# Half of the q transposes of an attention and MLP kernel as copies between partition halves

## The chip, the core and the metric

The kernel runs on one core of one Trainium2 chip. The metric is the device time of one execution in microseconds. A core has a matrix engine (TensorE, PE in the profile; its weight loads are PEld), a vector engine (VectorE, DVE), a scalar engine (ScalarE, ACT), GpSimd (POOL), and SyncE (SP), whose queue here only issues DMAs. POOL issues the loads from memory. Each engine works through its own instructions in their order; semaphores make one engine wait for another, or for a DMA. On chip, data lie in SBUF with 128 partitions, and TensorE writes to PSUM banks.

## The reference

Eight batches of 12 heads, 448 positions, head size 64; then an MLP on all 8 x 448 = 3584 rows:

```python
scores = scale * np.matmul(q, k.transpose(0, 1, 3, 2))     # scale = 1/sqrt(64)
attn = np.maximum(scores, 0.0) ** 2 / S                    # S = 448, no softmax
attn_out = np.matmul(attn, v)                              # (8, 12, 448, 64)
x = attn_out.transpose(0, 2, 1, 3).reshape(B * S, H * D)   # (3584, 768)
h = x @ w_in                                               # w_in (768, 2048)
g = 0.5 * h * (1.0 + erf(h * inv_sqrt2))
out = g @ w_out                                            # w_out (2048, 768)
```

All inputs and the output are fp32. The kernel computes with bf16 inputs of the matmuls.

## The kernel before

**Attention.** A batch is split into 3 head groups of 4 heads. For each group there are 7 QK steps of four quarter-array matmuls (64x64 tiles, 448 columns, into `ps`, L748). Each step's result is evicted with relu and the scale, by ScalarE (L760) or VectorE (L762), and squared on VectorE (L769) into `a_sq`. When the 7 steps of a group are there, 28 matmuls (AV, into `pav`, L809) multiply by v, and the result is cast into `xT`. Then come the MLP's matmuls: `psh` (L861), `pb` (L1005) and `pso` (L1178), with their sums on VectorE (`osb`, `part`, `s_sb`) and gelu on ScalarE. While attention of batches 2 to 7 runs, MLP pieces of earlier batches fill TensorE between its steps.

**How q and k come.** POOL loads k, q and v of a batch with a cast to bf16 into `nk`, `nq` and `v_sb`. From batch 2 on, one pair of buffers `nq` and `nk` serves all batches, so the loads of the next batch may start only when the present batch has been transposed out of them. v has three buffers. QK needs q and k with the head's 64 entries on the partitions. For batches 0 and 1 TensorE transposes them. For batches 2 to 7, SP issues DMA transposes (`add_T_dma`, the DMA at L660): from 128 columns of `nq` or `nk` to the 128 partitions of `qT` or `kT`, which have two buffers each; a batch's transposes wait for the QK of two batches before (`old_T`).

`qT` is a row of slots of 112 columns. A DMA transpose turns 128 columns, that is two blocks of 64, into one slot: one block on partitions 0 to 63, the next on 64 to 127. QK needs every block on both halves, since its quarter-array tiles read the lower or the upper half. So `nq` is transposed twice, from two starting points 64 columns apart: the even transposes fill the slots 1, 3, 5, ..., the odd ones the slots 0, 2, 4, .... With both, the upper half has block s in slot s, and the lower half block s - 1. Per batch there are 9 DMA transposes on SP, in the order kT, even, odd for each of the three groups. An odd one covers 8 or 9 slots and reaches into the next group, so it also waits for that group's q load (`beyond`).

**Gates.** POOL's loads of the next batch overwrite what the transposes read. POOL waits for them with a small copy from the transposed tile (`gate`, 128x16): `add_gate` for q of a group (L701), `add_kgate` for kT (L716), `add_vgate` for the last batch's v (L709). In each batch POOL has, in order: gate of group 0, kT gate of group 2, the v load of the batch after next, gate of group 2, and then the six loads of k and q. `war` gives these loads the transposes as predecessors.

**Order.** All instructions are recorded first as operations with the engines that may run them and estimated costs (`sch.add`). `ORDER` (L83 to 163) is a list of words, an engine's letter and an operation's number, which fixes for all operations on which engine and in which order they stand. It was made from a planner's costs; when the kernel is built it is only replayed. Stores of the output (L1139) stand in SP's queue between the transposes, each as two DMAs.

Of the kernel before, what the change touches and what calls it, by code (L numbers as in the profile page):

```python
# [92 lines left out]
P219 D220 A244 A258 A178 D200 P267 D191 P259 P210 G148 A179 S229 P204 D197 A184 G150 A268 P186  # L93
A260 D182 D187 P263 D215 A211 D188 P261 G151 A205 P207 A264 P216 S230 G153 D206 D185 D224 A262
A217 P192 A208 G154 D193 D194 D209 D212 P247 D221 A248 P255 P143 D218 A256 P201 P225 A144 A226
G237 D202 D203 P265 D227 D380 S231 D386 S232 P245 S233 A266 P362 A246 P372 A363 P370 A373 A371
D390 D388 P356 P366 A357 P368 A367 P376 D389 A369 A377 P358 P364 D383 D381 A359 A365 P360 P350
A361 P354 A351 P288 P282 D387 D384 A355 A289 P294 P378 A295 P374 P276 S234 A379 G240 D283 D284
D382 G149 P279 A375 P291 D280 D385 S235 P348 P352 P285 A292 A277 A349 D296 D290 D286 D287 A353
P306 P303 S236 P392 P300 D393 A304 P342 P394 D395 P396 P398 D391 A307 D281 A343 P312 P315 G152  # L100
A397 A301 A313 G155 G242 D278 D293 D316 G269 P297 G270 D399 G271 G272 P327 P400 D298 P402 D314
D302 D427 P324 A299 A328 S408 P309 D401 D403 P336 P404 A325 S409 A310 A337 P431 D305 D317 D326
G273 P318 A432 P339 P333 P435 D428 A334 G274 S410 D405 D311 P433 S411 S406 A340 P447 D319 A448
D344 D308 P462 D320 P321 G417 D434 P330 D429 P437 A322 A436 D329 D430 D335 A331 D341 P439 A323
S412 D338 D332 S413 P459 A463 P453 P345 A454 D460 D438 D440 S414 S415 P474 P465 D475 D455 G420
P441 P443 D442 A346 A466 P486 D444 A347 D467 G275 S416 P450 D451 A487 P456 D452 P531 G423 A532
D570 P547 A548 P549 P545 A550 D457 D571 S407 A546 P498 D464 P489 P504 D449 P529 D461 P523 A499
A490 P477 G418 D458 P480 D505 D478 A530 G419 P468 S551 G421 S552 A481 P471 A524 D476 D482 D469
D472 P483 D572 D473 P527 A484 D488 P537 A528 P533 D506 P510 G422 D485 A470 A538 D491 A534 P507
P501 S553 D500 A511 G424 P539 A502 A508 G425 S554 S445 P519 P625 G560 A626 P513 D479 A520 P492  # L110
P495 D514 D512 S555 P616 S556 S557 A540 D493 D515 P525 D496 A617 A494 G563 P535 P619 S558 D509
A526 D627 G426 S559 P613 A536 D614 G566 P610 P543 A544 D615 P541 D503 P521 D497 D573 G561 P640
A620 A611 P646 A641 D647 P516 D517 P634 A522 A542 D642 S446 P628 P574 A635 D629 P576 G562 P670
D612 S714 D621 D630 A518 S715 G564 P622 D618 G565 A575 P664 A623 A671 P578 D577 P580 P661 P637
A665 D624 D581 A638 P631 P649 D662 P676 A579 S716 D639 P582 P584 A632 D633 P652 A677 D583 A650
P667 D636 A653 D585 D651 S717 D648 A668 D654 P643 A644 G567 P586 S718 S588 D590 P594 P779 D645
D587 P673 P655 A780 G568 D592 D591 A595 P658 A674 P596 P782 D666 A659 S589 S719 D597 P773 A783
P598 A774 P600 D656 S720 P815 D663 P785 D675 A599 D657 P776 D669 D672 A786 G723 A777 A816 D601
G726 D660 D775 P602 D678 P604 P809 D735 D593 P791 S721 D603 D605 P679 A810 P806 P606 S722 D781
A680 S608 D778 P692 D607 D681 D792 A807 G569 A693 P706 P788 D787 P797 P824 A707 P686 A687 P704  # L120
D789 D790 G729 P702 D784 G724 P830 A798 S877 D793 A825 D817 P812 P794 G725 D831 A705 P803 A813
A795 D804 P836 D805 S878 S609 A703 G727 G728 A837 P708 A796 S879 D814 S880 P712 P833 D808 P839
D811 D733 P800 A709 P682 D801 A713 D802 D826 D799 A834 S881 A683 P700 G730 G731 D840 P696 A701
P688 S882 P925 P934 A935 P818 A689 D926 A697 P922 D832 P821 A819 P694 D734 D736 D923 D841 A820
G886 A695 A822 P710 S883 A711 D823 P827 P940 D828 G889 P931 D835 D829 P698 S884 A941 A699 D838
P690 A932 P684 D927 P919 G732 A691 P928 A685 D920 P842 D924 D936 A929 S885 P916 A843 A917 P949
P737 G892 G887 P739 D930 A950 P955 G888 D921 D844 S988 P943 S989 D933 G890 G891 A738 A956 D740
D918 D944 P964 P741 P743 A742 P745 D744 A965 D942 D746 P747 P749 P952 D753 D951 P946 S990 D748
D953 P937 D750 A947 G893 D954 P982 P958 D754 P757 A758 P759 P761 D957 S751 S991 D938 A959 A983
P997 A939 D960 P973 A998 D755 P979 G894 D760 D948 S992 P763 A762 A974 P765 D966 D764 D999 P767  # L130
P967 S752 S993 G1441 G895 D756 D766 D945 P976 A980 S994 A977 D975 D968 P961 P1015 A1016 P1027 D768
D896 D1028 P769 D770 P871 D962 S995 P855 D898 D981 D978 A872 A963 P970 D971 A856 D1017 P1036 D984
P1000 P865 A1001 P849 A866 A1037 P857 P1006 D972 P1024 D1002 A850 D969 P985 A1025 P1009 D1007 A858
P1012 D1077 P875 P869 A876 P861 A1013 S996 D897 A870 D986 A862 P873 D899 A874 A987 D1038 D1010
P847 S771 P1057 A848 P1030 P1003 D1008 D1011 A1031 P853 D1069 D1058 A1004 P863 D1014 P1063 D1029
D1005 A864 P1018 P1021 A854 D1064 P1045 P859 A1022 A1019 D1032 D1073 A860 D1074 P845 P867 P1039
D1070 A1046 A846 A1020 D1023 D1078 A868 P1051 P1033 P851 A1034 D1035 A852 A1040 P902 D1026 D1047
P900 A1052 D1065 P1048 A901 D1041 D1053 D1059 P1060 A1061 D903 P1042 P1054 A1043 A1049 D1079 D1080
P904 A905 D1044 D1071 P906 D1062 A1055 P908 P1081 D1151 D907 S772 D909 D1056 P1083 P1098 A1099
P1100 D1076 P912 P910 D1149 D1150 A1082 D1050 P1066 D913 D911 S914 D1084 S915 P1085 D1072 D1101  # L140
P1153 A1067 A1068 P1102 A1154 D1075 P1087 D1152 P1104 A1086 D1189 P1089 A1103 D1190 P1106 D1088
P1155 D1105 D1090 P1092 D1107 A1091 D1191 P1109 A1108 D1156 P1095 P1112 D1093 P1115 D1110 A1094
P1132 D1096 A1111 P1117 D1113 A1097 P1134 D1192 A1116 A1133 P1157 A1114 D1118 P1119 D1135 P1136
A1158 P1121 P1138 A1120 P1123 A1137 P1140 D1122 P1159 D1139 D1124 P1126 D1141 A1125 P1143 A1142
D1160 P1129 P1146 D1127 P1161 D1144 A1128 D1130 A1145 P1163 D1147 A1131 D1301 A1148 D1162 D1302
P1165 D1169 D1164 S1167 P1173 D1170 D1166 S1168 P1175 D1171 D1174 P1177 D1172 D1176 D1303 P1179
D1304 A1178 P1181 D1180 P1183 D1263 D1182 P1185 D1261 D1184 S1187 P1193 D1262 P1210 D1186 S1188
P1195 D1264 P1212 A1194 A1211 P1265 D1196 P1197 D1213 P1214 A1266 P1199 P1216 A1198 P1201 A1215
P1218 D1200 P1267 D1217 D1202 P1204 D1219 A1203 P1221 A1220 D1268 P1207 P1224 D1205 P1227 D1222
A1206 P1244 D1208 A1223 P1229 D1225 A1209 P1246 A1228 A1245 P1269 A1226 D1230 P1231 D1247 P1248  # L150
A1270 P1233 P1250 A1232 P1235 A1249 P1252 D1234 P1271 D1251 D1236 P1238 D1253 A1237 P1255 A1254
D1272 P1241 P1258 D1239 P1273 D1256 A1240 D1242 A1257 P1275 D1259 A1243 A1260 D1274 P1277 D1281
D1276 S1279 P1285 D1282 D1278 S1280 P1287 D1283 D1286 P1289 D1284 D1288 P1291 D1290 P1293 D1292
P1295 D1375 D1294 P1297 D1373 D1296 S1299 P1305 D1374 P1322 D1298 S1300 P1307 D1376 P1324 A1306
A1323 P1377 D1308 P1309 D1325 P1326 A1378 P1311 P1328 A1310 P1313 A1327 P1330 D1312 P1379 D1329
D1314 P1316 D1331 A1315 P1333 A1332 D1380 P1319 P1336 D1317 P1339 D1334 A1318 P1356 D1320 A1335
P1341 D1337 A1321 P1358 A1340 A1357 P1381 A1338 D1342 P1343 D1359 P1360 A1382 P1345 P1362 A1344
P1347 A1361 P1364 D1346 P1383 D1363 D1348 P1350 D1365 A1349 P1367 A1366 D1384 P1353 P1370 D1351
P1385 D1368 A1352 D1354 A1369 P1387 D1371 A1355 A1372 D1386 P1389 D1393 D1388 S1391 P1397 D1394
D1390 S1392 P1399 D1395 D1398 P1401 D1396 D1400 P1403 D1402 P1405 D1404 P1407 D1415 D1406 P1409  # L160
D1413 D1408 S1411 P1417 D1414 D1410 S1412 P1419 D1416 D1418 P1421 D1420 P1423 D1422 S1433 P1425
D1424 P1427 D1426 S1434 P1429 D1428 S1435 P1430 D1431 S1436 D1432 S1437
"""


class Op:

# [227 lines left out]
def kernel(  # L395
# [317 lines left out]
    def add_kgate(b, g):  # L713

        def fn(e):
            nc.gpsimd.tensor_copy(gate, get_T(b)[1][:, g, :: NK * 8])  # L716
# [803 lines left out]
```

## Time and profile before

| | us |
|---|---|
| median of 3 runs | 367.81 (367.30 to 368.25) |
| the profiled execution's own time | 369.13 |
| its span, first to last instruction | 367.3 |
| TensorE busy | 356.4 |
| VectorE busy | 286.5 |
| ScalarE busy | 201.6 |
| POOL busy | 65.1 |
| DMA transposes: qT 36, kT 18, median to landing | 4.0 |

Times in the profile are counted from the span's start. The share of busy time is an average over stages: up to some 57 us attention of batches 0 and 1 and the weights, from 57 to about 250 us attention of batches 2 to 7 between MLP pieces, and then the MLP alone. Matmuls overlap, so a busy TensorE is not always at its peak. In a chain or a list of waits, "DMA qT<-nq" is the landing of a transpose. An instruction's duration on VectorE and ScalarE overlaps a little with the next one's.

### The profile page before, as it was taken

The numbers are of one execution on the slowest core, as the hardware profiler recorded it, in microseconds if no ns is written. First come the engines' busy times: TensorE is split into PE (matmuls) and PEld (weight loads), VectorE is DVE, ScalarE is ACT, GpSimd is POOL, SyncE is SP. The second block draws the span as 40 slices with busy tenths as digits, with TensorE's granted clock in tenths as the row PEclk, the third lists the DMA queues.
The fourth block names the chain that finished last, engine by engine and source line by source line (L and its number), as shares of the span: only waits on it lengthen the run. The fifth ranks groups of instructions, "written<-read, shape, count | busy, mean of one in ns | idle before, by whom it ended". The sixth has DMA issues, their size and how long they took to land.

```text
span 367.3 us, 8386 instructions
## 1 busy us (share of the span) xinstructions
PE 356.4 (97%) x3517; PEld 218.4 (59%) x3517; DVE 286.5 (78%) x480; ACT 201.6 (55%) x319; POOL 65.1 (18%) x104
## 2 busy tenths in 40 slices
PE   7899999999999999899999999999999999999995
PEld 3566565455544454454455545467885897688663
DVE  3998887389899888688997898799778558755863
ACT  4997754676757676658672656763540353045200
POOL 8655700070150150060150100000000000000000
PEclk9999999999999999999999999999999999999999
DMA  9999999899999999999999970002002301310222
GB/s 169 200 202 204 202 204 187 172 161 188 177 175 188 188 181 148 230 168 214 179 159 193 186 169 2 0 2 73 15 2 87 87 2 34 95 46 0 87 86 86
DMA packets 89700, 47.25 MB, mean 129 GB/s; under 512 B 55360, under 2 KB 86336, under 8 KB 89664
## 3 DMA queue, kind: packets, MB, share of 16 engines
q0 software_dynamic: 32912, 22.47, 42.2%
q1 hardware_dynamic: 56112, 23.76, 33.8%
q8 instruction: 27, 0.44, 0.5%
q10 hardware_dynamic: 640, 0.51, 0.4%
q14 instruction: 9, 0.07, 0.1%
HBM read 45.61 MB, written 11.01 MB: 154 GB/s over the span
## 4 chain that ended last, share of the span: by engine, by line
PE 76%; DMA 10%; SPq 5%; DVE 5%; issue 1%; ACT 1%; POOL 1%; DVEq 0%; POOLq 0%
PE pso L1178 29%; PE psh L861 20%; PE pb L1005 13%; PE ps L748 7%; PE pav L809 6%; DMA nq<-in_q_dram 5%; SPq L660 4%; DMA qT<-nq 4%; DVE a_sq L769 2%; ACT a_sq L760 1%; DMA k<-in_k_dram 1%; DVE a_sq L762 1%; DVE osb L1212 1%; POOL nk L546 1%; SPq L1139 1%
## 5 line engine op out<-in xcount | busy, mean ns | idle before, releaser
L760 ACT ACTIVATE a_sq<-ps 128x896 bf16<-128x896 f32 (+1 forms) x122 | 106.9, 919 | 31.7 <-PE ps L748 31.2
L769 DVE TENSOR_TENSOR a_sq<-a_sq 128x896 bf16<-128x896 bf16 (+1 forms) x169 | 96.4, 614 | 2.8 <-ACT a_sq L760 2.4
L861 PE MATMUL psh<-xT,win_sb 128*128 128x448 bf16 (+1 forms) x516 | 95.7, 340 | 0.0
L861 PEld LDWEIGHTS <-win_sb 128*128 128x128 bf16 x516 | 48.2, 98 | 45.1 <-issue 8.9
L762 DVE TENSOR_SCALAR a_sq<-ps 128x896 bf16<-128x896 f32 (+1 forms) x47 | 50.6, 1076 | 20.1 <-PE ps L748 20.1
L1178 PEld LDWEIGHTS <-s_sb 128*128 128x128 bf16 x456 | 43.4, 98 | 29.9 <-issue 3.2
L871 ACT ACTIVATE h_sb<-psh 128x448 bf16<-128x448 f32 x80 | 43.3, 547 | 30.6 <-PE psh L861 30.4
L748 PE MATMUL ps<-qT,kT 64*64 64x448 bf16 (+1 forms) x756 | 47.6, 336 | 3.9 <-DMA qT<-nq 2.3
L1042 DVE TENSOR_TENSOR part<-pb,part 128x448 f32<-128x448 f32 x60 | 34.7, 619 | 21.1 <-PE pb L1005 21.1
L1178 PEld LDWEIGHTS <-h_sb 128*128 128x128 bf16 x336 | 32.0, 98 | 23.2 <-issue 3.5
L1178 PE MATMUL pso<-wout_sb,h_sb 128*128 128x384 bf16 x224 | 41.1, 326 | 0.0
L1178 PE MATMUL pso<-wout_sb,s_sb 128*128 128x384 bf16 (+2 forms) x232 | 41.1, 321 | 0.0
L1178 PE MATMUL pso<-t_sb,s_sb 128*128 128x384 bf16 x224 | 41.0, 326 | 0.0
L809 PE MATMUL pav<-a_sq,v_sb 64*64 64x448 bf16 (+1 forms) x756 | 36.6, 329 | 0.3 <-ACT a_sq L760 0.2
L1212 DVE TENSOR_TENSOR osb<-pso,p_sb 128x384 f32<-128x384 f32 x42 | 23.3, 554 | 15.7 <-PE pso L1178 10.5
L748 PEld LDWEIGHTS <-kT 64*64 64x64 bf16 x756 | 18.4, 105 | 25.3 <-issue 19.4
L1051 ACT ACTIVATE h_sb<-part 128x448 bf16<-128x448 f32 x36 | 20.1, 578 | 20.2 <-DVE part L1042 19.9
L1005 PEld LDWEIGHTS <-win_sb 128*128 128x128 bf16 x288 | 27.6, 98 | 2.3 <-issue 0.4
L809 PEld LDWEIGHTS <-v_sb 64*64 64x64 bf16 x756 | 21.5, 107 | 11.3 <-issue 1.2
L513 ACT CAST xT<-pav 128x448 bf16<-128x448 f32 (+1 forms) x31 | 15.3, 508 | 11.5 <-PE pav L809 9.8
L1005 PEld LDWEIGHTS <-ws 128*128 128x128 bf16 x216 | 20.7, 98 | 0.0
L1178 PE MATMUL pso<-t_sb,h_sb 128*128 128x384 bf16 x112 | 20.5, 326 | 0.0
(61 smaller groups left out, 266.8 us busy)
## 6 DMA issues: line engine op xcount, KB each, us to landing
nk<-in_k_dram POOLq DMA_DIRECT2D x23, 224.0 KB, 8.3
nq<-in_q_dram POOLq DMA_DIRECT2D x21, 224.0 KB, 9.3
v_sb<-in_v_dram POOLq DMA_DIRECT2D x5, 672.0 KB, 8.5
out_dram<-osb SPq DMA_DIRECT2D x7, 336.0 KB, 3.8
v_sb<-in_v_dram POOLq DMA_DIRECT2D x9, 224.0 KB, 7.6
out_dram<-osb SPq DMA_DIRECT2D x7, 288.0 KB, 3.0
out_dram<-osb SPq DMA_DIRECT2D x8, 240.0 KB, 3.7
win_sb<-in_moe_w_in_dram POOLq DMA_DIRECT2D x8, 192.0 KB, 8.6
```

The lines of the kernel that those rows point to most:

```text
L748: nc.tensor.matmul(ps[64 * j : 64 * j + 64, e, x * w : x * w + w], kT[r, g, i * 128 + 64 * j : i * 128 + 64 * j + 64], moving, start=True, ...
L760: A.activation(ar, ps, AF.Relu, scale=c_att)
L762: V.tensor_scalar(ar, ps, c_att, 0.0, op0=mybir.AluOpType.mult, op1=mybir.AluOpType.max,)
L769: V.tensor_mul(box["a2"][:, :, :used], ar, ar)
L809: nc.tensor.matmul(pav[0][o2 : o2 + 64, e, :w], vt[b][r, 2 * g + e, bass.ts(i, D)], box["a2"][r, y, o : o + w], start=(i == 0), stop=(i == ...
L861: nc.tensor.matmul(ph[:, x * n : x * n + n], win_sb[:, kd, bass.ts(m + x, 128)], xT[b][:, kd, c], start=(kd == 0), stop=(kd == KD - 1),)
L871: A.activation(h_ring()[:, m : m + nm, o + c.start : o + c.stop], box[0][:, :S].rearrange("p (x n) -> p x n", x=nm), AF.Gelu,)
L1005: nc.tensor.matmul(bank[name][:, y, z * HS : z * HS + HS], w[:, k, bass.ts(mm, 128)], right()[:, k], start=first and k == 0 and z == 0, st ...
L1042: V.tensor_add(get(to), ps(name), get(other))
L1051: A.activation(h_ring()[:, m : m + 2, o + half[c].start : o + half[c].stop], src().rearrange("p (x n) -> p x n", x=2), AF.Gelu,)
L1178: nc.tensor.matmul(box[bank][:, n0:n1], left()[:, kf], right()[:, kf, n0:n1], start=bool(need) and kf == 0, stop=kf == K2 - 1, skip_group_ ...
L1212: V.tensor_add(out()[:, n0:n1], box[bank][:, n0:n1], other()[:, n0:n1])
```

## The change

The odd transposes of batches 2 to 7 (3 per batch, 18 in all) are replaced. After the even transpose of a group, one operation of two copies moves what it brought: its upper half to the lower half of the next slots, and its lower half to the upper half of the slots before. Each copy has 64 partitions and 8 slots of 112 columns. The operation runs on VectorE or ScalarE as `ORDER` says: 10 pairs are on VectorE (all of batch 2, group 1 of batch 3, groups 0 and 1 of batch 4, groups 0 and 2 of batch 6, groups 1 and 2 of batch 7), and 8 on ScalarE. SP has 6 transposes per batch, kT and even for each group. QK now waits for the copies as well as for the even transpose.

The gates wait for even transposes only: the gate of a group reads what the even one wrote, and the v load of every batch now waits, in place of kT of group 2, for the even q of group 1. POOL's order stays. `war` leaves the copies out.

```diff
-            if bb == c and (b < 3 or g0 <= g < g1)
+            if bb == c and (b < 3 or g0 <= g < g1) and (c < 2 or o[0].mode == "X")
...
-        n0, odd = 0, None
+        def fill_halves(g):
+            def fn(e):
+                t = get_T(b)[0].rearrange("p (s t) -> p s t", t=KC)
+                n = 16 * g
+                copy(e, t[:64, n + 2 : n + 17 : 2], t[64:, n + 1 : n + 16 : 2])
+                copy(e, t[64:, n : n + 15 : 2], t[:64, n + 1 : n + 16 : 2])
+            return fn
+
         for g in range(G):
             op = turn(k_dst(g), k_src(g), list(ld_k[b, g]))
             for i in range(NK):
                 Tk[b, g, i] = (op, op)
             lands = list(dict.fromkeys(ld_q[b, g, c] for c in range(NC)))
-            n = 8 * g + 9
             even = turn(slots_of(8 * g, 1, 8), q_src(8 * g, 1, 8), lands)
-            prior = odd or even
-            beyond = [ld_q[b, g + 1, c] for c in range(NC)] if g < G - 1 else []
-            beyond = list(dict.fromkeys(beyond))
-            odd = turn(slots_of(n0, 0, n - n0), q_src(n0, 0, n - n0), lands + beyond)
-            n0 = n
-            for c, o in enumerate((even, odd, prior, odd)):
+            both = sch.add(
+                (("DVE", 1.0, 1.1), ("ACT", 1.6, 1.7)), fill_halves(g), [even] + old_T(b)
+            )
+            for c, o in enumerate((even, both, both, both)):
                 Tq[b, g, c] = (o, o)
...
-            n = (16 * g + 1) * KC
-            nc.gpsimd.tensor_copy(gate, get_T(b)[0][:, n : n + 16 * KC : KC])
-        deps = [Tq[b, g, c][0] for c in range(NC)] + [Tk[b, g, 0][0]]
+            n = (16 * g + 15) * KC
+            nc.gpsimd.tensor_copy(gate, get_T(b)[0][:, n : n + 16])
+        deps = [Tq[b, g, 0][0]]
...
     def add_vgate(b):
-            nc.gpsimd.tensor_copy(gate, get_T(b)[0][:, 32 * KC : 32 * KC + 16])
-        pool_q.append(sch.add((("POOL", 0.2, 0.3),), fn, [Tq[b, 1, 1][0]]))
+            nc.gpsimd.tensor_copy(gate, get_T(b)[0][:, 31 * KC : 31 * KC + 16])
+        pool_q.append(sch.add((("POOL", 0.2, 0.3),), fn, [Tq[b, 1, 0][0]]))
...
-    add_kgate(2, 2)
+    add_vgate(2)
...
-                        add_kgate(b + 1, 2)
+                        add_vgate(b + 1)
```

`ORDER` is another one from about 40 us on up to about 250 us: the number of matmuls and their kinds are the same, but MLP pieces stand in other places between QK and AV, and some evictions change their engine (relu of QK: 46 on VectorE and 121 on ScalarE before, 44 and 123 after). On SP, the first stores of the output stand in other places between the transposes: group 0's first store stood behind the fourth transpose of batch 3 and now stands ahead of that batch's last two.

More of the change, by code (lines that the diff above doesn't have):

```diff
@@ L98 @@
[L98 to L109, printed above, removed]
@@ L158 @@
[L158 to L162, printed above, removed]
+P219 D220 A244 A258 A178 P247 D197 D221 G148 A184 P261 D215 P207 S229 P210 D185 G150 A179 D208
@@ new lines @@
+A248 A262 P216 A217 D191 S231 P255 P263 A211 A256 G151 A264 P204 D209 A205 P186 D187 P192 D206
+D188 P259 A193 D224 A260 D194 P143 D200 D182 D218 P245 A144 P267 P201 D212 A246 P225 G153 A268
+P265 G154 D202 G237 D203 A226 D383 S232 G240 A227 A266 D388 P356 D380 G149 D384 D381 P378 A357
+P372 A379 G152 A373 P368 A369 P350 P354 A351 D389 A355 P366 D387 S234 P362 A367 G155 A363 P374
+A375 D382 S235 D386 P352 D390 D391 A353 P348 P364 G242 D230 D385 P294 P276 A349 D277 A365 P291
+A295 G269 P370 A292 P288 P279 P282 G270 A371 S408 D233 G271 P360 A280 D283 A361 P309 S409 G272
@@ new lines @@
+G273 P285 A286 D293 P358 P392 D284 S411 D310 A359 D296 D236 D287 A289 D393 D281 D278 P303 P318
+A319 P312 A313 D290 P394 A304 P396 P300 A301 S412 P306 D395 G274 A397 P297 A307 A298 P315 P376
+A316 D308 D302 P398 D317 A377 G417 P324 D311 D399 P333 D314 A299 P330 P400 P402 D305 D325 A334
+G420 P327 D401 P342 D427 D403 A331 D343 D320 P336 A328 A410 D329 P404 P431 D405 G275 A337 P456
+A457 P453 P321 S406 D335 S414 D428 S415 D332 P465 D326 A322 A432 G423 P433 A454 P435 D413 D434
+P339 G418 A466 D429 G419 D455 P483 S551 D338 D344 A323 A436 G421 S552 D430 A340 D341 P471 A484
@@ new lines @@
+P437 P439 A472 D438 P489 P474 A490 D440 D570 P345 P462 D346 D475 P441 P443 D347 D442 A463 D444
+S554 A416 P527 P447 P486 P450 A528 D473 A448 P541 G422 D487 A542 P531 D451 D571 P459 P480 D452
+G424 P501 D467 P543 A532 A544 D464 P545 A460 A546 D449 D476 P529 P525 D481 D458 A530 P477 D461
+A502 P468 D553 A526 A478 P495 P549 A496 P547 P628 A550 D572 P498 D482 D491 D469 A470 D485 D488
+A548 P504 P537 D629 A538 D505 A499 P535 D479 D506 P521 A536 P613 P622 P492 A522 A623 S555 S557
+D630 D614 G425 P625 P616 A617 P519 G560 P533 A626 P507 P619 D503 S558 D500 G563 A493 G426 D494
@@ new lines @@
+G566 D508 A520 P523 P510 P513 A534 A524 P574 D624 D509 S407 S445 A511 A620 G561 A575 G562 D514
+D512 D615 D618 P539 D497 P578 D556 G564 A540 D515 P576 P610 A611 P516 D577 P643 P649 D579 A559
+S714 P580 D517 D573 A644 A650 D518 P582 D627 S715 D581 D583 P637 D612 D645 P670 P640 A641 P584
+A638 A671 P586 P673 D621 S717 D585 D590 G565 A674 G567 P652 D642 P631 S718 D653 P661 D587 P634
+P594 A719 D591 S446 A632 G568 P596 D592 D635 P664 S720 D595 A662 A633 D654 A716 A665 D597 G723
+S588 D651 D636 P676 P646 A647 A677 D666 P598 P600 D599 D648 D678 D639 P602 D601 G726 P788 D789
@@ L708, in fn @@
         def fn(e):
-            nc.gpsimd.tensor_copy(gate, get_T(b)[0][:, 32 * KC : 32 * KC + 16])
-        pool_q.append(sch.add((("POOL", 0.2, 0.3),), fn, [Tq[b, 1, 1][0]]))
-    def add_kgate(b, g):
-        def fn(e):
-            nc.gpsimd.tensor_copy(gate, get_T(b)[1][:, g, :: NK * 8])
-        pool_q.append(sch.add((("POOL", 0.2, 0.3),), fn, [Tk[b, g, 0][0]]))
+            nc.gpsimd.tensor_copy(gate, get_T(b)[0][:, 31 * KC : 31 * KC + 16])
+        pool_q.append(sch.add((("POOL", 0.2, 0.3),), fn, [Tq[b, 1, 0][0]]))
     xT, hT = {}, {}
```

98 lines of the change are left out of this document (45 added, 53 removed).

## The prediction

> **What bounds the kernel now.** I read the busy shares first, then TensorE's waits, the stretches, the chain, and last the queues of SP and POOL and the prices of single instructions.
>
> ```profile
> PE 356.4 (97%) x3517; PEld 218.4 (59%) x3517; DVE 286.5 (78%) x480; ACT 201.6 (55%) x319; POOL 65.1 (18%) x104
> ...
> PE 76%; DMA 10%; SPq 5%; DVE 5%; issue 1%; ACT 1%; POOL 1%; DVEq 0%; POOLq 0%
> ```
>
> TensorE works 356.4 of 367.3 us. The chain's 10% DMA and 5% SP look like 50 us to be had, but a chain only names what came last. What can be given back is the time in which TensorE stands still for a transpose:
>
> ```profile
> PE ps L748 <- DMA qT<-nq: 2.3, 2, 1.6
> ```
>
> The stretches (length, then busy us and instructions of PE, PEld, DVE, ACT, POOL, then clock, DMA share, GB/s) say where: only 120 to 160 us has TensorE under 20.00. The other 9 us of idleness lie in the first 40 us and after the last matmul, which the change does not touch. The clock is 1.00 throughout.
>
> ```profile
> 60.00:80.00 20.00, 20.00 (x139) 9.67 (x138) 10.06 (x14) 12.84 (x20) 6.36 (x12) 1.00 1.15 165
> 80.00:100.00 20.00, 20.00 (x224) 10.82 (x222) 18.66 (x32) 13.12 (x18) 1.46 (x4) 1.00 1.20 182
> 100.00:120.00 20.00, 20.00 (x170) 9.63 (x162) 18.69 (x30) 13.51 (x21) 5.29 (x8) 1.00 1.25 177
> 120.00:140.00 20.00, 19.33 (x220) 10.24 (x218) 16.33 (x25) 13.80 (x23) 6.19 (x10) 1.00 1.11 192
> 140.00:160.00 20.00, 18.33 (x192) 9.75 (x184) 15.93 (x30) 13.16 (x17) 3.20 (x6) 1.00 1.11 172
> 200.00:220.00 20.00, 20.00 (x186) 10.51 (x182) 18.54 (x32) 11.99 (x18) 1.48 (x2) 1.00 0.97 187
> ```
>
> Note VectorE there: 18.5 to 18.7 of 20 in three stretches, half idle only at 60 to 80. That is the engine that gets most of the copies.
>
> **The change part by part.** All sums are against the profiled execution's span of 367.3 us. The median without a profile is 367.81, so I add a difference to 367.81.
>
> *The 18 odd transposes go: at most -2.3.* Each cost SP about 1.3 us of issue (18 x 1.29 = 23 us of SP's queue) and a place in the DMA rings, but TensorE saw only the 2.3 us: 0.67 us at 120.9 (batch 4's first QK) and 1.62 us at 148.0 (batch 5's). To see whether both go, I follow the loop of gates and transposes (POOL, then SP):
>
> ```profile
> 73.01 0.21 POOL L716 COPY gate<-kT 128x16 bf16<-128x16 bf16 x1 [4.97 <-DMA kT<-nk]
> ...
> 76.42 0.71 POOL L546 DMA_DIRECT2D nk<-in_k_dram  x1 [0.56 <-issue]
> ...
> 102.32 0.70 POOL L546 DMA_DIRECT2D nk<-in_k_dram  x1
> ```
> ```profile
> 66.92 2.64 SPq L660 DMA_TRANSPOSE qT<-nq  x2
> ...
> 89.77 1.24 SPq L660 DMA_TRANSPOSE kT<-nk  x1
> 91.11 1.00 SPq L1139 DMA_DIRECT2D out_dram<-osb  x2
> ```
>
> Batch 2's last transpose was the ninth; it is now the sixth. The sixth was issued at 68.3 and the ninth at 72.3, so the k and q loads of batch 3 leave 4.0 us sooner (72.4 for 76.42), and so do batch 3's transposes. Its fourth, now the last q of group 1, is issued near 85.8 (89.77 - 4.0) and lands 3.3 us later, as the sixth did (68.31 to 71.64; landings are the DMAs' last semaphore updates in the trace). Batch 4's v load follows that gate by 0.6, near 89.7. Here the new SP order matters: group 0's first store, which stood behind the fourth transpose, now stands ahead of batch 3's last two. SP is free for it at 87.1. Its data were ready at 87.2 before (the sum that ended at 87.20 on VectorE); with three pairs of copies ahead on VectorE, 3 x 1.1 = 3.3 us, at 90.5 at the latest. So the last q of batch 3 is issued at 89.4 to 92.8, to land at 92.7 to 96.1. But in the second case batch 4's v load is already moving, and the row for that is a store issued 0.8 us behind a v load (at 127.70): it landed at 136.35, with that load. A v load takes 9.6 us (99.73 to 109.31), so the last q would then land near 100.3. Batch 4's k and q loads leave 0.7 us later, at 93.4 to 101.0, where it was 102.32; its first q landed 16.1 us behind that (118.44), so 109.5 to 117.1, and with two copies 110.7 to 118.3.
>
> TensorE asks for it sooner, too. I counted the changed program's matmuls up to each batch's first QK and added the durations of the chain's pieces (0.189 for 448 columns, 0.163 for 384, 0.19 for four quarter-array QK). Before, they began at 69.1, 93.3, 120.9, 148.0, 178.0, 205.2 us; without waits they now stand at 68.9, 90.3, 116.6, 150.2, 181.7, 212.0. So for batch 4 the margin is -1.7 to 5.9 us. As the store comes nearer to 90.5 than to 87.2 by its place behind the copies, I take 0.7 us of a new wait. For batch 2 (66.9 landed, 1.1 of copies, 68.1) and 3 (86.8 + 1.8 on ScalarE, 88.6) it holds by 0.8 and 1.7. Batch 5's transposes need batch 3's QK out of the qT buffer, 127.3 by the same count, and its loads land by 137: q copied by 142, wanted at 150.2. By the same steps batches 6 and 7 have 8 us and more. The 1.62 us goes.
>
> *36 copies of 64x896 come: 20 on VectorE, 16 on ScalarE.* No row has an SBUF to SBUF copy.
>
> ```profile
> L769 DVE TENSOR_TENSOR a_sq<-a_sq 128x896 bf16<-128x896 bf16 x167 | 95.8, 617 | 2.8 <-ACT a_sq L760 2.4
> L762 DVE TENSOR_SCALAR a_sq<-ps 128x896 bf16<-128x896 f32 x46 | 49.9, 1086 | 20.1 <-PE ps L748 20.1
> L511 DVE COPY kT<-tp 128x896 bf16<-128x896 bf16 x4 | 2.5, 619 | 0.8 <-PE tp L605 0.8
> L511 DVE COPY qT<-tp 128x448 bf16<-128x448 bf16 x6 | 2.3, 385 | 0.0
> L513 ACT COPY qT<-tp 128x896 bf16<-128x896 bf16 x1 | 0.9, 911 | 0.0
> ```
>
> On VectorE the bounds are 385 ns (half the elements) and 1086 (as many, from fp32); I take 619, same operation, length and types. Back to back such instructions follow in 0.53 (the chain's a_sq pairs take 1.06), so 20 x 0.53 = 10.6 us. ScalarE: 911 to 950 (its cast of 512 SBUF elements took 618), back to back 0.80: 13 us. The new order moves two evictions from VectorE to ScalarE (46 to 44), -2 us. VectorE's idle time from 60 to 220 is 28 us (131.96 busy of 160), so the engine does not become the bound; but four of its ten pairs (batch 3 group 1, batch 4 group 0, batch 7 groups 1 and 2) fall where it idles 1.3 to 1.5 us in 20. These 8 x 0.53 = 4.2 us push back the squares and xT casts behind them, which AV and QK's banks wait for. Between 0 (all in gaps) and 4.2 I take 1.5, about a third, since two evictions leave and banks and a_sq are many. ScalarE idles 6 to 8 us in 20; nothing for it. A copy that waits for its landing blocks what is queued behind it: at 66.9 VectorE has nothing to do until 69.70; at batch 4 it is in the 0.7.
>
> The Trainium skill, "VectorE: DVE Perf Modes", section "The perf-mode tier table", says that such a copy runs at 4x. By its 58 + FD/4 cycles it would be an estimated 0.29 us, and my 1.5 would be some 0.8. The same page, "Two Vector instructions with no wait between them", says against the change that an instruction with another start quadrant is held until the earlier ones are finished; that would cost the 0.08 us of overlap three times a pair, and bring it back to 1.5. No row here shows either.
>
> *Order: +0.4.* TensorE changes between the 64x64 and the 128x128 arrangement 117 times before and 121 after. Eight QK matmuls take 0.38 behind AV and 0.50 behind pso, psh 2.38 behind QK and 2.27 behind pso:
>
> ```profile
> 164.59 3.51 PE psh L861 x18
> 168.10 0.50 PE ps L748 x8
> 168.60 1.32 PE pav L809 x28
> 169.93 0.38 PE ps L748 x8
> ```
>
> So 4 x 0.11. *Gates: 0.* Still 16 of 0.2 to 0.7 us on a POOL that waits 5 to 14 us before most of them; each waits for one transpose instead of up to five. Their gain is in the loop above. The stores' waits in SP (8 in the second half) hold only transposes with 8 us of margin.
>
> Sum: -2.3 + 0.7 + 1.5 + 0.4 = +0.3, so 367.81 + 0.3 = **368.1**.
>
> **The rivals.**
> - *Nothing new waits.* For: VectorE has 28 us of gaps, batch 4 may come 5.9 us ahead. Against: three stretches are full. 367.8 - 2.3 + 0.4 = 365.9 to 366.4.
> - *Copies at the price of the fp32 eviction* (1.0 back to back). For: strided slots, other partitions. Against: the 619 row. The 8 copies in full stretches then cost 8.0 in place of 4.2, and little of that fits: +3.4, 371.5. From about 0.75 each it outweighs the rest.
> - *Batch 4 still late.* If the store holds SP and the v load holds the rings, its q lands as before, 118.4; with copies 119.6 against 116.6: 3.0 in place of 0.7, 370.4. From a wait of 1.6 on it is slower by more than 0.3%.
> - *VectorE's copies and POOL block each other.* The copies of batch 2's groups 1 and 2 and one of batch 6 meet POOL's bursts of loads (0.71 to 0.76 each). At one such instruction per copy, batch 3's loads and so batch 4's come 1.2 later and wait that much more: 369.3. The Trainium skill, "SBUF — State Buffer", section "Who interferes with whom", has this rule for copies in two-port modes; no row here shows it.
>
> **How the numbers follow.** About 0.3% (1.1 us) is what a measurement of this kernel can tell from no change. Forecast 0.40 (367.0 to 368.9 its own range); nothing waits 0.20; dear copies 0.15; batch 4 late 0.17; POOL 0.08. Faster is the first rival, 0.20; same the forecast, 0.40; slower the other three, 0.40. The range 366.0 to 371.0 leaves out the fastest end of the first rival and most of the dear copies.
>
> **What would show it.** No TensorE wait at batch 5; a short one at batch 4, for VectorE's qT, not for a DMA; k and q loads of batches 3 and 4 issued near 72.4 and at 94 to 101; copies near 0.6 on VectorE and 0.9 on ScalarE; TensorE's waits for VectorE and ScalarE after 60 us near 1.5 in all. It is wrong if the copies take 1 us, or batch 4's first q lands after 117.

## The result

The changed kernel takes 369.42 us (median of 16 runs, 368.21 to 371.12), the kernel before 367.75 us beside it (16 runs, 366.20 to 373.44): ratio 1.0045, 95% interval 1.0024 to 1.0066, so it is slower by 0.9 to 2.4 us. Ratios and their intervals, here and below, leave out executions that took over 1.5% more than the fastest of their kernel. The forecast was 368.1 us with a range of 366.0 to 371.0, and held no measurable change (0.40) as likely as slower (0.40). In a second series, on another chip, the changed kernel took 368.92 us, and the ratio was 1.0038 (1.0018 to 1.0059).

The two profiles that stand against each other do not show this. The changed kernel's profiled execution took 369.21 us with a span of 367.4 us; that of the kernel before 369.13 us with 367.3 us. They differ by 0.1 us where the medians differ by 1.7. The profiled execution of before was 1.4 us above its own median. As far as the runs below show, that makes most of the forecast's error: some 1.0 of 1.3 us.

The profile after, in the order of the lines shown of before: the page's busy shares and the shares of its chain,

```profile
PE 357.7 (97%) x3517; PEld 217.8 (59%) x3517; DVE 294.2 (80%) x501; ACT 215.3 (59%) x334; POOL 63.6 (17%) x104
...
PE 85%; DVE 6%; DMA 4%; ACT 3%; issue 1%; SPq 0%; DVEq 0%; ACTq 0%
```

TensorE's waits from 40 to 270 us (us in all, times, the longest),

```profile
PE pso L1179 <- DVE osb L511: 0.7, 1, 0.7
PE ps L749 <- ACT xT L513: 0.3, 1, 0.3
PE pav L810 <- ACT a_sq L761: 0.3, 1, 0.3
```

and the stretches (length, then busy us and instructions of PE, PEld, DVE, ACT, POOL, then clock, DMA share, GB/s):

```profile
60.00:80.00 20.00, 19.95 (x149) 9.76 (x151) 15.70 (x24) 13.14 (x21) 7.28 (x12) 1.00 1.22 171
80.00:100.00 20.00, 19.70 (x202) 10.40 (x198) 16.86 (x31) 16.30 (x24) 1.23 (x3) 1.00 1.15 144
100.00:120.00 20.00, 19.67 (x180) 9.53 (x173) 16.80 (x28) 12.82 (x19) 6.17 (x12) 1.00 1.00 146
120.00:140.00 20.00, 20.00 (x191) 10.13 (x190) 16.54 (x29) 13.86 (x21) 5.21 (x9) 1.00 1.29 213
140.00:160.00 20.00, 19.29 (x191) 10.27 (x190) 18.26 (x32) 15.76 (x19) 4.79 (x8) 1.00 0.94 140
```

The reader is to see that no transpose stops TensorE any more: the 2.3 us of "DMA qT<-nq" are gone, the chain's DMA share fell from 10% to 4% and SP's from 5% to nothing. In their place stand three waits for VectorE and ScalarE, and TensorE, which was short of 20.00 by 0.67 and 1.67 in the last two of these stretches, now lacks 0.05, 0.30, 0.33 and 0.71 in four of them.

The prices of the copies, in the page's form (busy us, mean ns):

```profile
L770 DVE TENSOR_TENSOR a_sq<-a_sq 128x896 bf16<-128x896 bf16 (+1 forms) x169 | 97.2, 615 | 5.9 <-ACT a_sq L761 5.5
L511 DVE COPY qT<-qT 64x896 bf16<-64x896 bf16 x20 | 8.9, 443 | 5.2 <-DMA qT<-nq 4.8
L513 ACT COPY qT<-qT 64x896 bf16<-64x896 bf16 x16 | 15.0, 937 | 0.3
```

VectorE's copy has a median of 389 ns; a pair takes 0.81 us there, and 1.9 us on ScalarE.

Where TensorE stands still can be counted more finely than by the waits: for each matmul, the time to the next one's start, less what that kind takes when nothing waits (0.189 us for 448 columns, 0.163 for 384, 0.093 more for a switch of arrangement). What exceeds this by over 0.06 us I call the waits. From the 600th matmul (33 to 35 us, by the profile) to the last one's start:

| profile | own time | 600th to last matmul | waits in it | the rest |
|---|---|---|---|---|
| before, first | 369.13 | 329.00 | 2.54 | 326.46 |
| before, second | 366.81 | 326.95 | 0.49 | 326.46 |
| changed, first | 369.21 | 329.34 | 2.26 | 327.08 |
| changed, second | 367.86 | 328.75 | 1.68 | 327.07 |

The changed kernel's 2.26 are 0.22 at 77.6 us, 0.47 at 90.9, 0.50 at 118.0, 0.88 at 150.6 and 0.21 at 249.6; in the second profile those of 90.9, 150.6 and 249.6 come back with the same sizes, that of 118.0 is 0.13 and that of 77.6 is not there.

### The profile page after: what moved, and what is told of

The parts are those of the page before. It is cut to its first block, busy times and chain, and to the rows that moved or that the text cites. A ratio compares the mean times of both kernels' runs of the same rounds, so it can differ in the third digit from the quotient of the medians.

```text
span 367.4 us, 8405 instructions
## 1 busy us (share of the span) xinstructions
PE 357.7 (97%) x3517; PEld 217.8 (59%) x3517; DVE 294.2 (80%) x501; ACT 215.3 (59%) x334; POOL 63.6 (17%) x104
## 4 chain that ended last, share of the span: by engine, by line
PE 85%; DVE 6%; DMA 4%; ACT 3%; issue 1%; SPq 0%; DVEq 0%; ACTq 0%
PE pso L1179 32%; PE psh L862 22%; PE pb L1006 13%; PE ps L749 8%; PE pav L810 8%; ACT a_sq L761 2%; DVE a_sq L770 2%; DMA qT<-nq 2%; DVE a_sq L763 1%; DVE qT L511 1%; DMA k<-in_k_dram 1%; ACT qT L513 1%; DMA out_dram<-osb 1%; PE tp L605 0%; PE tp L633 0%
## 5 line engine op out<-in xcount | busy, mean ns | idle before, releaser
L761 ACT ACTIVATE a_sq<-ps 128x896 bf16<-128x896 f32 (+1 forms) x124 | 108.6, 923 | 20.9 <-PE ps L749 20.3
L763 DVE TENSOR_SCALAR a_sq<-ps 128x896 bf16<-128x896 f32 (+1 forms) x45 | 48.1, 1075 | 8.2 <-PE ps L749 8.0
```

The source lines that it names most:

```text
L761: A.activation(ar, ps, AF.Relu, scale=c_att)
L763: V.tensor_scalar(ar, ps, c_att, 0.0, op0=mybir.AluOpType.mult, op1=mybir.AluOpType.max,)
```

## The experiments

The medians are of 6 or 12 runs; every ratio is against runs of the kernel before on the same chip, whose medians were 367.64 to 368.41. The profile is of one of the runs, and its own time says how typical that one is.

| run | median us | the profiled run's time | ratio, 95% interval |
|---|---|---|---|
| before_again | 367.73 | 366.81 | 0.9996 (0.9958 to 1.0034) |
| before_third | 371.0, one run | 371.0 | |
| after_again | 368.92 | 367.86 | 1.0038 (1.0018 to 1.0059) |
| order_only | 374.41 | 373.16 | 1.0184 (1.0129 to 1.0239) |
| copies_only | 384.75 | 386.71 | 1.0412 (1.0339 to 1.0486) |
| copies_gaps | 370.11 | 370.53 | 1.0049 (1.0019 to 1.0079) |
| copies_slim | 367.92 | 369.47 | 1.0003 (0.9970 to 1.0035) |
| act_moved | 368.54 | 367.84 | 1.0003 (0.9970 to 1.0035) |
| all_moved | 368.14 | 367.97 | 0.9991 (0.9963 to 1.0020) |
| b2_copies | 367.48 | 366.68 | 0.9997 (0.9977 to 1.0018) |
| b23_copies | 369.19 | 367.42 | 1.0050 (1.0025 to 1.0075) |
| old_gates | 396.44 | 395.95 | 1.0743 (1.0682 to 1.0804) |

Two questions lead through them. First: was the profiled execution of before typical (theory A) or a slow one (theory B)? Second: what do the copies cost, the place in a queue where a pair stands (place theory), or the engine time (load theory)?

**The kernel before, twice more (before_again, before_third).**

> The kernel before, unchanged. Theory A (the profiled execution of before is typical): its span is again near 367.3 us, TensorE waits 2 us or more for qT at batches 4 and 5. Theory B (that execution was a slow one, since its own time of 369.13 us is 1.4 above the median of 367.75): the span comes out near 366.0 and the waits of batches 4 and 5 near 1 us in all. The ratio is 1.000 within 0.3% by both.

> The kernel before, unchanged, a third profile. If the waits of batches 4 and 5 differ from execution to execution (2.5 us in the first profile, 0.5 in the second), the span follows them at about 1 us per us: 364.4 plus the waits.

TensorE's waits from 40 to 270 us in the second profile, and in the third:

```profile
PE ps L748 <- issue: 0.3, 1, 0.3
```
```profile
PE ps L748 <- DMA qT<-nq: 2.7, 2, 2.5
```

The same kernel waits 0.3, 2.3 or 2.7 us for the same two transposes. The second profile's span is 364.9 us, as theory B said, and the table above shows that the first and second differ in nothing but the waits and 0.3 us before 34 us: 326.46 us in both without them. Taking the waits from the two own times leaves 366.6 and 366.3; the median of 367.75 so stands for some 1.3 us of waits. That is an estimate: it takes the first 34 us as these two profiles have them, and in the 14 profiles of this document the 600th matmul starts anywhere from 33 to 35 us. Theory A falls.

The spread comes by way of the loop. Batch 3's first transpose was issued at 83.3 us in the first profile and 82.5 in the second, batch 4's loads at 102.3 and 101.2, batch 4's first transpose at 110.6 and 108.2, batch 5's at 137.8 and 135.6 (81.7, 101.3, 110.2 and 138.3 in the third): each round of loads and transposes waits for the one before, and what a load lost is carried on. Why the loads themselves take longer in one execution than in another, the traces do not show.

In the third profile the wait was long enough for a second loss. TensorE's own lines and the stretches around them:

```profile
148.39 0.57 PE L748 MATMUL ps<-qT,kT 64*64 64x448 bf16 x8 [2.45 <-DMA qT<-nq]
148.77 2.71 PE L809 MATMUL pav<-a_sq,v_sb 64*64 64x448 bf16 x28
```
```profile
146.00:148.00 2.00, 0.00 (x0) 0.00 (x0) 2.00 (x5) 0.00 (x0) 0.00 (x0) 1.00 0.52 112
148.00:150.00 2.00, 1.61 (x24) 1.20 (x28) 0.30 (x1) 1.18 (x3) 0.21 (x1) 0.73 1.13 238
150.00:152.00 2.00, 2.00 (x21) 0.88 (x14) 0.00 (x0) 1.04 (x3) 0.00 (x0) 0.50 0.96 295
152.00:154.00 2.00, 2.00 (x17) 0.83 (x16) 0.39 (x1) 0.92 (x2) 0.00 (x0) 0.91 0.97 207
```

After 2.45 us of standing still the granted clock fell to 0.50, and the 28 AV matmuls took 2.71 us, which take 1.52 at the same place in the two other profiles. The table's rest is 328.1 us here, 1.6 more than in the other two. The span was 369.1; "364.4 plus the waits" gives 367.2, and the half clock 1.6 of the remaining 1.9.

**The order alone (order_only).** The code of before with the changed `ORDER`; the odd transposes stay DMAs:

```diff
-S408 S409 S411 S412 S406 S414 S415
+S408 S409 S410 S411 S412 S413 S406 S414 S415 S416
...
-A410 D413 A416
```

> The new order alone: the odd transposes stay DMAs, each right behind its even one in SP's queue, and the old gates stay; every other instruction stands as in the changed kernel. Theory A and B: batch 4 is asked for at 116.6 us, 4 us sooner than before, while its q comes as late as before (118.4) or later, so TensorE waits 2 to 4 us there, and nothing at batch 5 (asked at 150.2): 367.75 + 0.4 for the switches + 2 to 4 less what batches 4 and 5 cost before (2.3 by A, 1 by B): 368 to 370 by A, 369 to 371 by B. A rival, that the order alone makes the changed kernel's loss and the copies nothing: 369.4 with no wait at batch 4.

It took 374.41 us, more than any theory gave. The waits came, but in other places than batch 4's first QK:

```profile
PE ps L746 <- DMA qT<-nq: 3.6, 2, 2.3
PE pso L1176 <- DVE osb L1210: 1.3, 1, 1.3
PE pso L1176 <- DVE osb L509: 0.6, 1, 0.6
```

The 3.6 us are batch 3's first QK at 91.8 us and the first of batch 5's group 2 at 163.5; VectorE's osb waited 2.4 us at 150.5 for a store that stood behind the transposes. The new order asks for q sooner, and needs the shorter queue. The rival that the order alone makes the whole loss is not excluded by this run. The table of waits excludes it: the rest is 326.9 to 327.1 us with the new order (order_only among them) and 326.5 with the old one, and this 0.6 us (with the 0.2 at 249.6, which every run with the new order has) is what the order costs.

**The copies with the old order, placed by landing (copies_only), and by gaps (copies_gaps).** TensorE's, the stores' and POOL's words of before; the pairs' words (batch 4's as the example):

```diff
-S553
-S556
-S559
+D553 D488
+D556 D496
+A559 A544
```
```diff
+D553 D500
+A556 A544
+D559 D647
```

> The copies and the new gates with the old order: TensorE's sequence, the stores and POOL's order stand as in the kernel before, SP has six transposes per batch, and the 36 copies stand on the same engines as in the changed kernel, where their data land. Theory A: the waits of batches 4 and 5 go, 2.3 us, and the copies cost 0.5 to 1.5: 366 to 367. Theory B: only 1 us of waits is there to go, so 367.3 to 368.3.

> The copies with TensorE's old order once more, now each pair in an idle gap of VectorE (14 pairs) or ScalarE (4 pairs) of the kernel before, between the landing and the first QK of its group. The place theory: the transposes' waits of batches 4 and 5 go whole, no switches are added, and the pairs cost 0 to 0.5: 366.2 to 366.9. The load theory: 14 pairs of 0.8 us are 11 us more on VectorE, whose free time lies in gaps of under 1 us; 367.8 to 369.5.

Placed where the old profile had the data land, less some microseconds for the earlier loads, the copies cost 15 us by the ratio. VectorE, in its own lines, and TensorE's longest waits:

```profile
222.13 0.79 DVE L509 COPY qT<-qT 64x896 bf16<-64x896 bf16 x2 [6.51 <-DMA qT<-nq]
222.95 0.56 DVE L1211 TENSOR_TENSOR osb<-pso,p_sb 128x384 f32<-128x384 f32 x1
```
```profile
PE pso L1177 <- DVE osb L1211: 5.2, 2, 4.5
```

The pair of batch 7 stood at the head of VectorE's queue 6.5 us before its data, and the sum behind it, which TensorE wanted, stood with it. That run tells what a wrong place costs and nothing else. In gaps, the waits for transposes were gone, but the time was 370.11, over 3 more than the place theory gave, and 0.6 above the load theory's range. Waits from 40 to 270 us:

```profile
PE ps L747 <- DVE a_sq L761: 1.0, 3, 0.4
PE pav L808 <- DVE a_sq L768: 0.3, 1, 0.3
PE pav L808 <- DVE a_sq L761: 0.2, 1, 0.2
```

By the spacing of the matmuls it is nine waits of 0.1 to 0.6 us, 3.05 in all; the rest is 326.6, the old order's. So the load theory is the better one there, though its range was passed too: VectorE's short gaps are not free time that can be filled. The waits are for evictions and squares on VectorE, which, as I read it, come later by what a pair overhangs its gap.

**The copies made small (copies_slim).**

```diff
-                tpool.tile([128, SLOTS * KC], BF16, tag="qT", name="qT"),
+                qkT[b - 2][0] if b >= 4 else tpool.tile([128, SLOTS * KC], BF16, tag="qT", name="qT"),
...
+                w = KC if b < 4 else 4
-                copy(e, t[:64, n + 2 : n + 17 : 2], t[64:, n + 1 : n + 16 : 2])
-                copy(e, t[64:, n : n + 15 : 2], t[:64, n + 1 : n + 16 : 2])
+                copy(e, t[:64, n + 2 : n + 17 : 2, :w], t[64:, n + 1 : n + 16 : 2, :w])
+                copy(e, t[64:, n : n + 15 : 2, :w], t[:64, n + 1 : n + 16 : 2, :w])
```

> The changed kernel with the 24 copies of batches 4 to 7 cut from 112 columns of a slot to 4 (their output is left incomplete; the waits stay): 12 on VectorE cost some 0.3 us less each, 12 on ScalarE some 0.7 less each. If the copies' time on the engines makes the loss, as at 150.6 us, where TensorE stands 0.7 us behind a pair on ScalarE: 0.7 to 1.5 us less than the changed kernel, 368.0 to 368.7. If the loss is the order's and the waits': 369.2 to 369.5.

This kernel leaves out 108 of the 112 columns, so its result is not the product; it is there for the time alone. It took 1.5 us (0.42% by the ratios) less than the changed kernel, the upper end of what the copies' side gave: with the copies of batches 4 to 7 made short, the loss is all but gone. The two intervals taken together give this difference 0.39% either way, and against the second series of the changed kernel it is 0.35%, so the times alone barely tell it. TensorE's waits from 40 to 270 us:

```profile
PE ps L750 <- ACT xT L513: 1.5, 1, 1.5
PE pav L811 <- ACT a_sq L762: 0.3, 1, 0.3
```

The wait at 150 us is gone. That at 118 us was 1.6 us in this execution, one of the slowest of its twelve, since batch 4's q landed at 116.5; that at 90.9, behind a pair of batch 3 that kept its length, stayed.

**Pairs moved (act_moved, all_moved).** To see whether that loss lies in the engine time or in the place:

```diff
 A674
-A719
+A716
 A632
...
 A633
-A716
 A665
...
 A677
+A719
 A786
```
```diff
 D395
+D236
 D308
...
+D410
 D343
...
 D553
+D469
 D572
```

> The changed kernel with two pairs of copies moved in ScalarE's queue: batch 5's group 0 from ahead of the evictions at 149.6 us to 143.9, where group 1's stood, and group 1's behind those evictions. The place theory (a pair costs only where it stands ahead of evictions or casts that TensorE waits for: 0.2 us at 77.6, 0.5 at 90.9, 0.5 at 118.0, 0.9 at 150.6 in the changed kernel's trace): the wait at 150.6 goes, 369.42 - 0.9 = 368.5. The load theory (what the copies take of VectorE and ScalarE costs, wherever they stand): the wait comes back behind the next evictions, 369.4.

> The same, and three more moves: batch 2's group 2 on VectorE from 75.4 us to its gap at 80, batch 3's group 0 from ScalarE to VectorE ahead of its eviction at 88.3, and the cast of pav that ScalarE's second cast waits for to the place right behind batch 4's first pair. The place theory: all four waits go, 369.42 - 2.1 = 367.3 to 367.8 (0.4 for the switches is still in it). The load theory: 369 or more.

The place they left, in the changed kernel's trace from 147 to 152 us:

```profile
147.67 1.88 ACT L513 COPY qT<-qT 64x896 bf16<-64x896 bf16 x2
...
149.58 2.54 ACT L761 ACTIVATE a_sq<-ps 128x896 bf16<-128x896 f32 x3
150.53 0.63 DVE L770 TENSOR_TENSOR a_sq<-a_sq 128x896 bf16<-128x896 bf16 x1 [1.03 <-ACT a_sq L761]
151.07 0.55 DVE L511 COPY osb<-pso 128x384 f32<-128x384 f32 x1
...
151.67 1.14 PE L1179 MATMUL pso<-t_sb,s_sb 128*128 128x384 bf16 x6 [0.71 <-DVE osb L511]
```

It reads as a relay: ScalarE's pair holds the eviction, the eviction holds VectorE's square, and the square holds the copy of a bank that TensorE wants next. The pair was batch 5's group 0, landed at 135.8 and not wanted before 153.1. TensorE's waits from 40 to 270 us with the two pairs moved, and with all of them:

```profile
PE pav L808 <- ACT a_sq L759: 0.3, 1, 0.3
```
```profile
PE ps L747 <- ACT a_sq L759: 0.3, 1, 0.3
PE pso L1177 <- DVE s_sb L1158: 0.3, 1, 0.3
```

Moved, the wait for `osb` is gone. The time of 368.54 is the 368.5 expected, but in part by luck: the kernel before stood at 368.39 on this chip, so that by the ratios the gain is 0.42% or 1.5 us (again with 0.39% either way), and in that profile the wait at 118 was absent too. The three further moves gave 0.4 more where 0.7 to 1.2 were expected: the waits at 77.6 and 90.9 went, and two of 0.4 and 0.5 us came at 92.2 (for `s_sb` on VectorE) and 174.2 (for an eviction on ScalarE). So both theories have a part: a pair in a bad place costs up to 0.9 us, and where an engine has no slack the move brings a smaller wait elsewhere. all_moved is 2.0 us faster than the changed kernel (0.54% by the ratios, with 0.35% either way) and not to be told from the kernel before.

**One batch's copies in the kernel before (b2_copies, b23_copies).**

```diff
+COPIED = (2,)
...
-            odd = turn(slots_of(n0, 0, n - n0), q_src(n0, 0, n - n0), lands + beyond)
+            if b in COPIED:
+                odd = sch.add(
+                    (("DVE", 1.0, 1.1), ("ACT", 1.6, 1.7)), fill_halves(g), [even] + old_T(b)
+                )
+            else:
+                odd = turn(slots_of(n0, 0, n - n0), q_src(n0, 0, n - n0), lands + beyond)
...
-            nc.gpsimd.tensor_copy(gate, get_T(b)[0][:, n : n + 16 * KC : KC])
+            w = 15 if b in COPIED else 16
+            nc.gpsimd.tensor_copy(gate[:, :w], get_T(b)[0][:, n : n + w * KC : KC])
```

> The kernel before with one part of the change: only batch 2's three odd transposes are replaced by pairs of copies, on VectorE, where it has 8 us of idle time up to 69.5 us; order, gates and the transposes of batches 3 to 7 stay. If the loop of gates and transposes sets when batches 4 and 5 come, batch 3's loads leave up to 4 us sooner and every later batch with them, so that the waits at 120 and 146 us go in every execution, at no cost: 364.9 us of span less the 0.5 of waits in it, 366.3 to 366.8, and none of the runs above 369. If the waits come from each batch's own queue instead: 367.5 to 368.4, with the same upper tail as before.

> The same with batch 3's three pairs too (two on VectorE, one on ScalarE, where they stood in the run with the old order and idle gaps). With the waits already gone these can only cost: in that run's trace TensorE waited 0.8 us at 100 to 102 us behind them. By the place theory with nothing to gain: 0.3 to 0.9 more than with batch 2 alone. If earlier loads still gain: the same or less.

With batch 2 alone the loop moved: batch 3's loads left at 73.5 us (76.4 in the first profile of before), batch 4's first transpose at 106.5 (110.6). The waits of 120 and 146 us were gone, one of 0.6 us stood at 151.3 for a later transpose of batch 5 (0.1 there in both profiles of before), and the rest was 326.46. The 12 runs lie between 366.49 and 368.83, where those of before reach 370, but the median gained only 0.2 us. Of the 1.3 us of theory B some 0.8 were left to gain beside that new wait; the interval of the ratio ends at a gain of 0.8. So this run allows 1.3 us for the median's waits, at its edge, and speaks for less; the gain is mostly in the long executions. Batch 3's pairs then lost 1.7 us, not the 0.3 to 0.9 expected, and not only by what they take. The profile with both is of the fastest of its twelve executions and has 0.8 us more of waits than that with batch 2 alone; where the other 0.9 of the median lie, no trace shows. POOL, in the trace with both:

```profile
103.46 0.62 POOL L715 COPY gate<-qT 128x15 bf16<-128x15 bf16 x1 [7.12 <-ACT qT L512]
```

The old gate waits for the copies. Those of group 2 stood in ScalarE's gap at 101.5, the loads of batch 4 left at 104.0 instead of 99.3, and TensorE waited 0.8 us for batch 4's transpose again.

**The gates undone (old_gates).**

```diff
...
-            n = (16 * g + 15) * KC
-            nc.gpsimd.tensor_copy(gate, get_T(b)[0][:, n : n + 16])
+            n = (16 * g + 1) * KC
+            nc.gpsimd.tensor_copy(gate[:, :15], get_T(b)[0][:, n : n + 15 * KC : KC])
-        deps = [Tq[b, g, 0][0]]
+        deps = [Tq[b, g, c][0] for c in range(NC)] + [Tk[b, g, 0][0]]
...
-                        add_vgate(b + 1)
+                        add_kgate(b + 1, 2)
```

> The changed kernel with the old gates: POOL's gate of a group waits for kT and for all of the group's q, the copies with it, and the v load waits for kT of group 2 again, in place of the even q of group 1. In the changed kernel batch 3's last even q landed at 100.9 us and batch 4's k and q loads left at 101.6, while that group's copies stand on ScalarE from 102.4 to 104.3. If the gates are part of the loop that sets when batch 4 comes, its loads now leave at 104.6 or later, its q lands some 3 us later against a QK asked for at 117.8, and VectorE, whose pair for it stands ahead of squares and casts, is held as long: 369.4 + 2 to 4, 371.4 to 373.4. If the gates are worth nothing, as the prediction costed them: 369.0 to 369.6.

396.44 us: 27 us slower than the changed kernel, far beyond both numbers. POOL and TensorE in that trace:

```profile
147.19 0.21 POOL L707 COPY gate<-qT 128x15 bf16<-128x15 bf16 x1 [20.54 <-ACT qT L511]
147.73 0.70 POOL L544 DMA_DIRECT2D nk<-in_k_dram  x1 [0.33 <-issue]
```
```profile
168.29 1.34 PE L754 MATMUL ps<-qT,kT 64*64 64x448 bf16 x12 [11.38 <-ACT a_sq L766]
```

Batch 4 lost some 4 us, as expected. What was not foreseen is batch 5: the pair of batch 4's group 2 stands late in ScalarE's queue (it ran at 145 us), since its QK is late; with the old gates batch 5's loads wait for it, and left at 147.7 where they leave at 120.0 in the changed kernel. ScalarE's copy for batch 5 then stood in front of evictions until q landed, TensorE waited 11.4 us, and its clock averaged 0.74 from 160 to 180 us. The gates are what allows the copies to stand late.

## Why the prediction was right and wrong

The time lies inside the range of 366.0 to 371.0 and outside the forecast's own 367.0 to 368.9. Term by term:

- *"The 18 odd transposes go: at most -2.3."* **This is the term that put the forecast off.** The mechanism was right: both waits went. But 2.3 us (2.54 by the spacing) was one execution's, 1.4 us above the median, and I subtracted it from the median. Three profiles of the kernel before have 0.49, 2.54 and 2.84 us; the two own times and the median put the median's share near 1.3, and with batch 2's copies alone less than that was gained. How much the median execution of before waits was not measured directly. With -1.3 the sum is +1.3, against +1.7 measured.
- *The loop, 4.0 us sooner.* Right up to batch 4's loads. POOL's lines:

```profile
72.27 0.70 POOL L546 DMA_DIRECT2D nk<-in_k_dram  x1 [0.58 <-issue]
...
89.12 0.84 POOL L564 DMA_DIRECT2D v_sb<-in_v_dram  x1 [0.32 <-issue]
101.03 0.20 POOL L709 COPY gate<-qT 128x16 bf16<-128x16 bf16 x1 [11.07 <-DMA qT<-nq]
101.56 0.70 POOL L546 DMA_DIRECT2D nk<-in_k_dram  x1 [0.34 <-issue]
```

  72.4 and 89.7 were foretold, and 93.4 to 101.0 for batch 4's loads, which left at 101.56. So the later end of the range came: the store did hold SP (issued at 88.41), and batch 3's last q, issued at 90.66 behind the v load, landed at 100.90, 0.8 after that load. Batch 4's q landed at 114.75, inside 109.5 to 117.1, and the rival "batch 4 still late" fell. It fell with some luck: q landed 13.2 us behind the first load, where I had taken the 16.1 of the kernel before, which would have made it 117.7.
- *Batch 4, +0.7.* 0.50 and 0.13 in the two profiles, but not by the mechanism I gave, TensorE waiting for VectorE's `qT`. From 114 to 119 us:

```profile
114.84 0.81 DVE L511 COPY qT<-qT 64x896 bf16<-64x896 bf16 x2 [1.63 <-DMA qT<-nq]
...
117.39 0.61 DVE L511 CAST xT<-pav 128x448 bf16<-128x448 f32 x1
...
118.08 0.53 ACT L513 CAST xT<-pav 128x448 bf16<-128x448 f32 x1 [0.74 <-DVE xT L511]
...
118.67 0.38 PE L749 MATMUL ps<-qT,kT 64*64 64x448 bf16 x4 [0.33 <-ACT xT L513]
```

  The copies were in time (QK at 117.77). VectorE had stood 1.63 us for the landing, and the cast queued behind the pair, `s_sb` and two squares came late; ScalarE waited for that cast and TensorE for the bank. I had named this kind of harm ("blocks what is queued behind it") and then booked it on `qT` alone.
- *Copies, +1.5, all of it on VectorE; "ScalarE idles 6 to 8 us in 20; nothing for it".* The sum was right, 1.57 and 1.35 us in the two profiles, and the engine wrong, so the sum was luck. ScalarE's pairs made 1.35 of it (0.47 at 90.9, 0.88 at 150.6), VectorE's 0.22. The prices were off the same way: 389 ns for 619 on VectorE, 937 with no overlap for 800 on ScalarE. A share of idle time in 20 us says nothing of the 1.9 us ahead of an eviction.
- *Order, +0.4.* 0.6 by the table, of which four more switches at 0.093 are 0.4, and a wait of 0.2 at 249.6 that every run with the new order has.
- *Gates, 0.* Right as they stand in the change; old_gates shows what they hold up.
- *Rivals.* "Dear copies" is excluded by the price. "VectorE's copies and POOL block each other" is half right: four of the 20 copies took 608 to 720 ns, each while POOL issued loads, as here,

```profile
75.37 1.40 DVE L511 COPY qT<-qT 64x896 bf16<-64x896 bf16 x2
...
75.80 0.76 POOL L467 DMA_DIRECT2D nq<-in_q_dram  x1
```

  and the wait of 0.22 at 77.6 us comes behind this pair (in the second profile it took 1.2 us and no wait followed). POOL's side was hardly touched: its issues beside copies kept their 0.70 to 0.76 us, but for one of 0.87 at 173.0 in place of 0.74, and the loads were not late. The Trainium skill, "SBUF — State Buffer", "Who interferes with whom", says that a copy in a two-port mode and GpSimd block each other for a whole instruction; this trace agrees that they disturb each other, but two other copies beside such issues kept 387 and 390 ns. The Trainium skill, "VectorE: DVE Perf Modes", "The TRN2 errata", says of the 58 + FD/4 cycles that they come out too low, and that a fixed part of some 150 cycles was measured; with that, and its 0.96 GHz, an estimate for 896 elements at 4x is 0.39 us, and the 389 ns agree. The Trainium skill, "VectorE: DVE Perf Modes", "Two Vector instructions with no wait between them", agrees as well: a copy starts 13 to 31 ns after the end of the one before, where the squares overlap by 0.08 us.

The new terms (order 0.6 + 0.2, copies 1.57, batch 4 0.50) are 2.9 us against 2.6 forecast, less some 1.3: +1.6, and 1.67 was measured. By the second profile (0.6 + 0.2, 1.35, 0.13) they are 2.3, which gives +1.0; so the account closes to some 0.6 us, and no better.

## What to carry to other kernels

A wait that hangs on DMAs in a loop can differ from execution to execution (0.5, 2.5 and 2.8 us here). Before it is subtracted from a median, see whether the profiled execution is itself at the median (its own time against the runs shown), and take the excess off the wait first. The same holds for the profiles of experiments: several here are of the fastest or the slowest execution of their run. An engine's idle share does not price an added instruction: ask what stands next in its queue, and which buffer the matrix engine waits for at the end of that relay. Where copies take the place of DMAs, what waits for the DMA alone (the gates here) must not come to wait for the copies, and a copy that waits for a landing must not stand ahead of an eviction.

## What the hardware showed that I had not expected

TensorE's granted clock fell to 0.50 for 3.4 us after it had stood still for 2.45 us (the third profile of before), at a cost of 1.6 us; after 2.33 us in order_only it stayed at 1.00, and after 1.6 in the first profile of before too.

The 14 traces together tell more. Between its first rise and the end of the work, the granted clock was at 1.00 or 0.50 for whole numbers of steps of 3.41 us (in the third profile of before 42 steps, then 1, then 63), and how long TensorE stood still within one such step tells when it fell. From 1.00 it fell after each of the seven steps with 1.74 us or more (one in the third profile of before, two in copies_only, four in old_gates) and after none with 1.62 or less (the largest are 1.62 in the first profile of before and 1.54 in order_only). The 2.33 us of order_only lay across the edge of two steps, 0.79 in one and 1.54 in the next. So a wait of over some 1.7 us, half a step, may cost the clock or not, by where it falls. The Trainium skill, "TensorE: Matmul & The Clock Gate", Part 1, names an idle window of some 3.4 us for it; here about half of one was enough.

That a wait of 2.5 us can so cost 4 may be why the kernel before has runs of 370 us and more. Of its 25 runs above 369.8 beside the experiments, 20 show a mean granted clock of 0.993 to 0.995; of the 80 below, 72 show 0.998 to 1.000. Only one trace of such a run was taken, so this is an inference.
